# Gradient of x in a transformer block's backward: token-major against transposed accumulation, with DMA transposes back

## The chip, the cores and the metric

The kernel runs on one core of a Trainium2 chip. The time is device microseconds from launch to end, the median of several runs. The engines are named as in the profile: PE (TensorE, with its weight loads as PEld), DVE (VectorE), ACT (ScalarE), POOL (GpSimd) and SP (SyncE, which here only issues DMAs). ACT and POOL issue DMAs too, each from its own instruction queue, in order with its other work.

## The reference

One block of a transformer, forward and gradients, in bf16: S = 2048 tokens, D = 640, H = 32 heads, F = 1728.

```python
h  = x + attn(layernorm(x), wqkv, wo)     # linear attention, phi(t) = elu(t)+1
h2 = h + swiglu(layernorm(h), w1, w3, w2)
out, vjp = jax.vjp(f, x, wqkv, wo, w1, w3, w2)   # f gives h2
return out, *vjp(grad_out)                # out_0 and the gradients out_1 .. out_6
```

The change lies in `out_1`, the gradient of x. With g_q, g_k and g_v the gradients of q, k and v, and `wqkv = [wq wk wv]`:

```
g_xn = g_q wq^T + g_k wk^T + g_v wv^T          # 2048 x 640
dx   = layernorm_backward(g_xn; xn, rs) + g_h  # per token: two sums over 640, then elementwise
```

## The kernel before

Tokens lie in 16 tiles of 128 (ST = 16), the width D in 5 pieces of 128 (DT = 5); W = 512 tokens, or TPC = 4 tiles, are a chunk, of which there are SC = 4. `manual_schedule` keeps the instructions of each engine in the order of the source. A tile framework adds all semaphore waits from the reads and writes of each tile. Every step of PE, ACT, DVE, POOL and SP named below therefore runs in source order on its own engine, and waits at the head of its queue.

The kernel works in stages: forward, gradients of the second half of the block, then from about 560 us the backward of the attention. Those that bear on the change:

- The stage of g_k (L1434 to L1455, PSUM tiles `dkv`) makes `g_kT`, the gradient of k with D on the partitions. In its gaps PE does the weight gradient of q as ten `jobs` (L1357, `grad_halves` L1338): 16 matmuls each with `xnN` (the normalised x, tokens on partitions) as weights, an eviction by ACT into a piece of `obs` (L1348), a DMA out by POOL (`dmaG`).
- SP's queue before the stage of x holds DMA transposes of weights and activations (`load_xnT`, `load_pkT`, `load_wqT`), and five `e_T` (L1423 to L1425, issued at L1456): each turns one token tile of g_q (128 x 640) into a slot of `bd`.
- The stage of x (L1506 to L1517), for each of the 16 token tiles t: `e_gxn(t)` (L1489) accumulates over 15 pieces of 128 (5 of g_q from `bd`, 5 of g_k from `g_kT`, 5 of g_v from `pkT`), with the token tile as weights and 320 columns of `wqT` moving, once for each half of D, so 30 matmuls (L1495) into a two-bank PSUM tile, of which there are two. Then `ln_bwd` (L1138): ACT copies the PSUM to bf16 `gs` and sums it on the way (L1143), DVE forms the second sum and `wb` (L1146 to L1151), ACT makes `y` (L1155), DVE adds `g_h` (L1156). After that SP issues `e_T(t+5)` into the slot that PE has just left, two `k_turn` (L1485 to L1487: a DMA transpose of a 128 x 512 tile of `g_kT` into four token tiles of `g_k`, 20 in all), and the write of the 128 x 640 result (L1513). In the last tiles SP also loads the normalised h, `hn`, into `g_q` (L1483, four quarters), and the first block `gb` of the gradients of gate and up, turned by DMA (L1475, in three parts).
- After the loop ten more jobs (the weight gradient of k, with `g_k` moving) run on PE, in two PSUM banks (`njob = 2`), and their outputs leave by SP.
- The last stage (L1541 to L1549) makes the gradients of w1 and w3, 35 jobs with `hn` as weights and `gb` moving; ACT evicts each and issues its DMA, for the first six in two halves (L1547).

`ln_bwd` is shared with an earlier stage of 16 tiles (L1159), where `gs` isn't given. In that stage, between 410 and 523 us, ACT issues DMA transposes (L1168, L1268); everywhere else SP issues them.

Of the kernel before, what the change touches and what calls it, by code (L numbers as in the profile page):

```python
# [9 lines left out]
P = 128  # L10
BF16 = mybir.dt.bfloat16
F32 = mybir.dt.float32
ALU = mybir.AluOpType
AF = mybir.ActivationFunctionType
AX = mybir.AxisListType
# [5 lines left out]
ST, DT = S // P, D // P  # L21
FT, FP = 14, 1792
FL = F - 13 * P
W, SC, TPC = 512, 4, 4
HD = D // 2
NG = 27
NB = 496
# [28 lines left out]
def kernel(  # L56
# [19 lines left out]
    V, A, T, G, SY = nc.vector, nc.scalar, nc.tensor, nc.gpsimd, nc.sync  # L76
    dma, dmaT, dmaG = SY.dma_start, SY.dma_start_transpose, G.dma_start
# [8 lines left out]
    out1S = rows(out_1.flatten_outer_dims())  # L86
# [16 lines left out]
    r_v, pk_v, xn_v, hn_v, m_v, pq_v = rows(r_d), rows(pk_d), rows(xn_d), rows(hn_d), rows(m_d), rows(pq_d)  # L103
# [24 lines left out]
    bd = cp.tile([P, DT, D], BF16, name="bd")  # L128
# [44 lines left out]
    ln1, ln2 = Stats("ln1"), Stats("ln2")  # L173
# [5 lines left out]
    ps = pool("p1p", space=PSUM)  # L179
# [348 lines left out]
    for t in range(ST):  # L528
        first = None
        if t < RAW:  # L530
# [11 lines left out]
            k = p1_mm(t, D, between, kh)  # L542
            act(0, 1)
            act(1, 1)
        else:
            k = p1_mm(t, D, (lambda: p1_tr(t + 1)) if t + 1 < XT_DMA else None)
# [97 lines left out]
    ps = pool("pap", space=PSUM)  # L644
# [351 lines left out]
    for c in range(SC):  # L996
# [9 lines left out]
        for fc in range(FT):  # L1006
# [8 lines left out]
            if c == 0 and fc in (5, 7, 9, 11):  # L1015
                a, b = {5: (0, 3), 7: (3, 6), 9: (6, 10), 11: (10, 13)}[fc]
# [13 lines left out]
            if c == SC - 1 and fc in (1, 2, 5, 6):  # L1030
                i = (1, 2, 5, 6).index(fc)
# [29 lines left out]
    ps = pool("pcp", space=PSUM)  # L1061
# [18 lines left out]
    for n in range(len(blk) * DT):  # L1080
        b, m = divmod(n, DT)
        f0, fw = blk[b]
        tag = "gw0" if n // 4 in (0, 2) or n in (16, 17) else "gw1"
        acc = ps.tile([P, 512], F32, name="gw", tag=tag, bufs=4)
        for t in range(ST):
            T.matmul(acc[:, 0:fw], lhsT=g2[:, t, m * P:(m + 1) * P], rhs=hb[b][:, t, 0:fw], start=(t == 0),  # L1086
                     stop=(t == ST - 1))
# [18 lines left out]
    g_h, g_n = g_hx[:, :, G0:G0 + D], g_hx[:, :, G0 + D:]  # L1106
    n_hi = H - M_H[3][0]
    g_q = bl.tile([P, ST, D], BF16, name="g_q")
    bo = pool("bo")
    r_sb = bo.tile([P, ST, D], BF16, name="r_sb")  # L1110
    ps = pool("pbp", space=PSUM)
# [25 lines left out]

    def ln_bwd(acc, t, nrm, st, out, res, pl, gs=None, y=None):  # L1138

        if gs is None:  # L1140
            gs = pl.tile([P, D], BF16, name="gs", bufs=2)
        s = pl.tile([P, 4], F32, name="s", bufs=2)
        A.activation(out=gs[:].rearrange("p (j n) -> p j n", j=2), in_=acc[:, :, 0:HD], func=AF.Identity,  # L1143
                     accum_out=s[:, 0:1])
        wb = pl.tile([P, D], F32, name="wb", bufs=2)
        V.scalar_tensor_tensor(out=wb[:], in0=gs[:], scalar=1.0, in1=nrm, op0=ALU.mult, op1=ALU.mult,  # L1146
                               accum_out=s[:, 1:2])
        V.tensor_scalar(out=s[:, 2:3], in0=s[:, 1:2], scalar1=-1.0 / D, scalar2=None, op0=ALU.mult)
        V.tensor_scalar(out=s[:, 3:4], in0=s[:, 0:1], scalar1=-1.0 / D, scalar2=st.rs[:, t:t + 1],
                        op0=ALU.mult, op1=ALU.mult)  # L1150
        V.scalar_tensor_tensor(out=wb[:], in0=nrm, scalar=s[:, 2:3], in1=gs[:], op0=ALU.mult, op1=ALU.add)  # L1151

        def rest():
            yt = pl.tile([P, D], BF16, name="y") if y is None else y
            A.activation(out=yt[:], in_=wb[:], func=AF.Identity, bias=s[:, 3:4], scale=st.rs[:, t:t + 1])  # L1155
            V.tensor_tensor(out=out, in0=yt[:], in1=res, op=ALU.add)  # L1156
        return rest
# [72 lines left out]
    xnN = g2  # L1230
# [4 lines left out]
    xnT, pkb, gb = {}, {}, {}  # L1235
# [10 lines left out]
    for t in range(ST):  # L1246
        g = b_ghn(t)
# [13 lines left out]
        if t >= 1:  # L1261
# [3 lines left out]
            if t <= 2 * DT:  # L1265
                n = (t - 1) % DT
# [24 lines left out]
    a, b = ST - 1, ST - 2  # L1291
# [4 lines left out]
    wqT = U1.tile([P, 15, D], BF16, name="wqT", tag="D")  # L1296
# [22 lines left out]
    pkT = bv.tile([P, DT, S], BF16, name="pkT")  # L1319
# [10 lines left out]
    obs = U1.tile([P, OB], BF16, name="obs", tag="MW")  # L1330
# [3 lines left out]
    def grad_job(lhs, m, rhs, n, out, q=dma):  # L1334
        for _ in grad_halves(lhs, m, rhs, n, out, q):
            pass

    def grad_halves(lhs, m, rhs, n, out, q=dma):  # L1338

        acc = ps.tile([P, 512], F32, name="job", bufs=njob)  # L1340
        for t in range(ST):
            if t == ST // 2:
                yield
            T.matmul(acc[:, 0:n], lhsT=lhs[:, t, m * P:(m + 1) * P], rhs=rhs(t), start=(t == 0),  # L1344
                     stop=(t == ST - 1))
        ob = obs[:, cnt[0] % (OB // n) * n:(cnt[0] % (OB // n) + 1) * n]
        cnt[0] += 1
        A.copy(out=ob, in_=acc[:, 0:n])  # L1348
        for x, y, to in out:
            q(out=to, in_=ob[:, x:y])  # L1350

    def half(src, j):
        return lambda t: src[:, t, j * HD:(j + 1) * HD]

    gqkv = {0: g_q}

    def wq_jobs(ks):  # L1357
        for m in range(DT):
            for k in ks:
                for j in range(2):  # L1360
                    yield from grad_halves(xnN, m, half(gqkv[k], j), HD,
                                           [(0, HD, out2S[:, m, k * D + j * HD:k * D + (j + 1) * HD])],
                                           dma if k else dmaG)
                    yield

    ps.release()
    ps = pool("pdp", space=PSUM)
# [18 lines left out]
    def fill(n):  # L1386
        for _ in range(n):
            next(jobs, None)

    fill(4)  # L1390
    for m, (a, b) in enumerate(M_H):
        n = (b - a) * DH
        acc = ps.tile([P, 512], F32, name="gkvT", tag="dkv", bufs=3)
        for c in range(DT):
            T.matmul(acc[:, 0:n], lhsT=woT[:, c, m * P:(m + 1) * P], rhs=QT[:, c, a * DH:b * DH], start=(c == 0),
                     stop=(c == DT - 1))
# [8 lines left out]
    g_kT = bs.tile([P, DT, S], BF16, name="g_kT")  # L1405
    dx = pool("dx")
    gm, gkv_b = (dx.tile([P, DT, D], BF16, name=n) for n in ("gm", "gkv_b"))
    g_k = gqkv[1] = U1.tile([P, ST, D], BF16, name="g_k", tag="S0")
# [11 lines left out]

    gT = {}

    def e_T(t):  # L1423
        gT[t] = bd[:, t % DT, :].rearrange("p (k q) -> p k q", q=P)
        dmaT(out=gT[t], in_=g_q[:, t, :])  # L1425

    mN = U1.tile([P, DT, D], BF16, name="mN", tag="W6")
    load_pkT(2)
# [5 lines left out]
    for n in range(0, SC * DT, 2):  # L1434
        pair = [divmod(i, DT) for i in (n, n + 1)]
        acc = d_acc()
        for b, (c, d) in enumerate(pair):
            for k in range(DT):
                T.matmul(acc[:, b, :], lhsT=gm[:, k, d * P:(d + 1) * P], rhs=xnT[c][:, k, :], start=(k == 0),  # L1439
                         stop=(k == DT - 1))  # L1440
        for b, (c, d) in enumerate(pair):
            cs = slice(c * W, (c + 1) * W)
# [6 lines left out]
        if 8 <= n < 8 + 2 * DT:  # L1449
# [3 lines left out]
            ob = obs[:, k * D:(k + 1) * D]  # L1453
            unload(sq, ob)
            dmaG(out=out2S[:, i, 2 * D:3 * D], in_=ob)  # L1455
    for t in range(DT):  # L1456
        e_T(t)
    for _ in jobs:
        pass
    dx.release()  # L1460
    ba.release()


    ex = pool("ex", "right")
    hnN = g_q
    blocks = [(f0, min(f0 + NB, 2 * F)) for f0 in range(0, 2 * F, NB)]
    NB0 = 160

    def load_block(i, a=0, b=NB):
        if i < len(blocks):  # L1470
            f0, f1 = blocks[i]
            if a == 0:
                gb[i] = ex.tile([P, ST, NB], BF16, name="gb", bufs=2)
            b = min(b, f1 - f0)
            dmaT(out=gb[i][:, :, a:b], in_=gg_d[f0 + a:f0 + b, :])  # L1475
# [4 lines left out]
                for lo, out in ((0, out4S), (F, out5S)) if max(f0, lo) < min(f1, lo + F)]  # L1480

    def load_hnN(i):
        dma(out=hnN[:, i * TPC:(i + 1) * TPC, :], in_=hn_v[:, i * TPC:(i + 1) * TPC, :])  # L1483

    def k_turn(n):  # L1485
        c, d = divmod(n, DT)
        dmaT(out=g_k[:, c * TPC:(c + 1) * TPC, d * P:(d + 1) * P], in_=g_kT[:, d, c * W:(c + 1) * W])  # L1487

    def e_gxn(t):  # L1489
        acc = ps.tile([P, 2, 512], F32, name="gxn", tag="gxn", bufs=2)  # L1490
        for j in range(2):
            for k in range(15):
                ts = slice(t * P, (t + 1) * P)
                g = gT[t][:, k, :] if k < DT else g_kT[:, k - DT, ts] if k < 2 * DT else pkT[:, k - 2 * DT, ts]
                T.matmul(acc[:, j, 0:HD], lhsT=g, rhs=wqT[:, k, j * HD:(j + 1) * HD], start=(k == 0),  # L1495
                         stop=(k == 14))
        gx = scr[:, t % 2, :]
        ln_bwd(acc, t, xnN[:, t, :], ln1, gx, g_h[:, t, :], ex, scr[:, 2 + t % 2, :], scr[:, 4, :])()
        return gx

    ps.release()
    ps = pool("pep", space=PSUM)
    njob = 2
    jobs = wq_jobs((1,))
    scr = U1.tile([P, DT, D], BF16, name="scr", tag="W6")
    for t in range(ST):  # L1506
        gx = e_gxn(t)
        if t + DT < ST:
            e_T(t + DT)
        for n in (2 * t, 2 * t + 1):  # L1510
            if n < SC * DT:
                k_turn(n)
        dma(out=out1S[:, t, :], in_=gx)  # L1513
        if t > 10 and t < 15:
            load_hnN(t - 11)
        if t in (11, 13, 15):
            load_block(0, (t - 11) // 2 * NB0, (t - 9) // 2 * NB0 if t < 15 else NB)  # L1517
    load_block(1)
    for _ in jobs:
        pass  # L1520
# [20 lines left out]
    for i, (f0, f1) in enumerate(blocks):  # L1541
        n = f1 - f0
        for m in range(DT):
            last = (i, m) == (len(blocks) - 1, DT - 1)
            for a, b in ((0, n - P), (n - P, n)) if last else ((0, n),):
                c = (a + b) // 2
                halves = ((a, c), (c, b)) if i * DT + m < 6 else ((a, b),)  # L1547
                out = [(x + y - a, z + y - a, to) for y, w in halves for x, z, to in both_grads(m, f0 + y, f0 + w)]
                grad_job(hnN, m, lambda t: gb[i][:, t, a:b], b - a, out, A.dma_start)  # L1549
        load_block(i + 2)  # L1550
        if 0 < i <= 4:
            gw2_out(i - 1)
        if i < 4:
            gw2_turn(i)
# [37 lines left out]
```

## Time and profile before

| | us |
|---|---|
| median of 3 runs | 820.39 (820.0 to 820.97) |
| the profiled execution, whole | 819.31 |
| its span, first to last instruction | 817.3 |
| PE starts the stage of x | 610.84 |
| PE starts the ten jobs on g_k | 676.04 |
| PE starts the last stage | 697.77 |
| end of ACT's last issue | about 815.3 |

In the stage of x (611 to 676 us) PE is busy for all of it, DVE for 37.1 us and ACT for 25.7 us. The granted TensorE clock is full throughout. In SP's queue, the transposes of L1425 and L1487 each hold the queue for 1.2 to 1.3 us. The profile's PE times for one instruction contain its latency; the pace of a stream is read from the starts.

In the excerpts below, "L1495 PE MATMUL a<-b,c" is a line of the kernel, an engine, an operation, and what it writes and reads; "x160 | 27.0, 299 | 0.0" are count, busy us, mean ns, and idle us before. "x1, 2.5" at a DMA is the count and the median us from its issue to its landing.

### The profile page before, as it was taken

What the parts mean: (1) busy time and instruction counts of PE and PEld (TensorE: products, weight loads), DVE (VectorE), ACT (ScalarE), POOL (GpSimd) and SP (SyncE); (2) the same over time, 40 slices, a digit from 0 to 9 for tenths busy, and PEclk for the clock granted to TensorE, in tenths of its full rate; (3) what the DMA queues carried; (4) which work ended last, traced back from release to release, by engine and by line L of the source; (5) the groups of instructions that cost most, each with busy time, mean ns of one, the idle gap of its engine ahead of it and who ended that gap; (6) DMA issues with size and microseconds to landing.
All of it is one profiled execution on the core that took longest, in us unless ns stands there. A gap on an engine that the chain in (4) does not pass through costs nothing.

```text
span 817.3 us, 13571 instructions
## 1 busy us (share of the span) xinstructions
PE 812.6 (99%) x5227; PEld 495.2 (61%) x5227; DVE 444.9 (54%) x976; ACT 324.4 (40%) x607; POOL 128.6 (16%) x194
## 2 busy tenths in 40 slices
PE   9999999999999999999999999999999999999998
PEld 6777544555555555754577777777657777544444
DVE  7859997998898566300057777772565551000000
ACT  7856688665565666011122212222113442111111
POOL 2243333323222212100001111110120000000000
PEclk9999999999999999999999999999999999999999
DMA  9799899696485556999867887259995679679991
GB/s 257 210 241 283 207 264 317 203 243 175 125 211 154 169 173 168 227 263 239 242 176 182 211 198 199 58 114 180 214 184 104 122 166 255 177 179 233 239 220 38
DMA packets 334480, 159.83 MB, mean 196 GB/s; under 512 B 252304, under 2 KB 327920, under 8 KB 334416
## 3 DMA queue, kind: packets, MB, share of 16 engines
q1 hardware_dynamic: 290976, 119.37, 62.7%
q0 software_dynamic: 7008, 23.17, 8.4%
q10 hardware_dynamic: 36432, 16.42, 8.2%
q8 instruction: 41, 0.67, 0.3%
q14 instruction: 23, 0.19, 0.1%
HBM read 44.47 MB, written 53.43 MB: 120 GB/s over the span
## 4 chain that ended last, share of the span: by engine, by line
PE 98%; DVE 1%; ACT 0%; DMA 0%; POOL 0%; issue 0%
PE mm L395 21%; PE job L1344 20%; PE ghn L1131 14%; PE gxn L1495 8%; PE gw L1086 7%; PE big L268 4%; PE o L913 4%; PE o L859 3%; PE gwo L1219 3%; PE macc L430 3%; PE at L657 3%; PE gr L1188 3%; PE dkv L1439 3%; PE mm L268 1%; PE dkv L1378 1%; PE gp L395 1%
## 5 line engine op out<-in xcount | busy, mean ns | idle before, releaser
L1344 PE MATMUL job<-gb,g_q 128*128 128x496 bf16 (+3 forms) x576 | 116.8, 366 | 0.0
L1131 PEld LDWEIGHTS <-ggb 128*128 128x128 bf16 x864 | 84.5, 98 | 33.0
L395 PE MATMUL mm<-pqT,w 128*128 128x512 bf16 x405 | 93.6, 379 | 0.0
L1344 PEld LDWEIGHTS <-g_q 128*128 128x128 bf16 x576 | 55.8, 98 | 61.0
L395 PEld LDWEIGHTS <-w 128*128 128x128 bf16 x540 | 52.6, 98 | 63.0 <-issue 0.8
L1348 ACT CAST obs<-job 128x496 bf16<-128x496 f32 (+4 forms) x56 | 28.6, 511 | 136.5 <-PE job L1344 126.0
L1131 PE MATMUL ghn<-w13a,ggb 128*128 128x320 bf16 x448 | 63.5, 299 | 0.0
L1131 PE MATMUL ghn<-w13b,ggb 128*128 128x320 bf16 x416 | 61.4, 299 | 0.0
L1146 DVE SCALAR_TENSOR_TENSOR wb<-gs,hnb 128x640 f32<-128x640 bf16 x16 | 13.2, 825 | 88.1 <-ACT gs L1143 88.1
L395 PE MATMUL mm<-g2T,w2T 128*128 128x512 bf16 x240 | 59.6, 379 | 0.0
L1086 PE MATMUL gw<-hb,g 128*128 128x512 bf16 (+2 forms) x320 | 58.6, 346 | 0.0
L1086 PEld LDWEIGHTS <-g 128*128 128x128 bf16 x320 | 31.3, 98 | 26.9
L420 ACT CAST ghh<-mm 128x512 bf16<-128x512 f32 x48 | 28.1, 585 | 47.6 <-PE mm L395 41.2
L1196 POOL TENSOR_TENSOR sz<-Zb,g_h 128x640 f32<-128x640 bf16 x16 | 20.2, 1261 | 163.6 <-DVE g_h L1197 163.6
L796 ACT ACTIVATE sig<-mm 128x512 bf16<-128x512 f32 x56 | 33.7, 602 | 25.2 <-PE mm L395 21.7
L1143 ACT ACTIVATE gs<-ghn 128x640 bf16<-128x640 f32 x16 | 11.2, 703 | 77.1 <-PE ghn L1131 77.1
L395 PEld LDWEIGHTS <-w2T 128*128 128x128 bf16 x260 | 25.4, 98 | 23.4
L268 PEld LDWEIGHTS <-pqT 128*128 128x128 bf16 x320 | 30.7, 98 | 13.5 <-ACT pqT L260 0.9
L1344 PEld LDWEIGHTS <-g 128*128 128x128 bf16 x320 | 31.0, 98 | 12.8
L268 PE MATMUL big<-wqkv,pqT 128*128 128x320 bf16 x250 | 38.5, 299 | 0.2
L832 DVE TENSOR_TENSOR gate<-gate,sig 128x1024 bf16<-128x1024 bf16 x28 | 19.3, 689 | 33.8 <-ACT gate L807 31.1
L1091 ACT CAST gw2o<-gw 128x512 bf16<-128x512 f32 (+2 forms) x20 | 10.4, 519 | 65.5 <-PE gw L1086 25.5
(212 smaller groups left out, 1378.1 us busy)
## 6 DMA issues: line engine op xcount, KB each, us to landing
hh_d<-hhT SPq DMA_DIRECT2D x24, 256.0 KB, 2.8
gg_d<-gate POOLq DMA_DIRECT2D x24, 256.0 KB, 4.4
gg_d<-ghh POOLq DMA_DIRECT2D x24, 256.0 KB, 4.1
ggb<-gg_d SPq DMA_DIRECT2D x6, 896.0 KB, 5.4
ggb<-gg_d ACTq DMA_DIRECT2D x6, 832.0 KB, 5.6
ggb<-gg_d SPq DMA_DIRECT2D x2, 1728.0 KB, 12.6
x_sb<-in_A_x_dram SPq DMA_DIRECT2D x4, 640.0 KB, 5.1
pk_d<-pk_all SPq DMA_DIRECT2D x4, 640.0 KB, 5.7
```

Source lines behind the costliest of these rows:

```text
L268: T.matmul(acc, lhsT=pqT[:, c, t * P:(t + 1) * P], rhs=wqkv[:, c, n0:n0 + HD], start=(c == 0), stop=(c == DT - 1))
L395: T.matmul(acc[:], lhsT=w[:, c, fc * P:(fc + 1) * P], rhs=rhs[:, c, :], start=(c == 0), stop=(c == DT - 1))
L420: A.copy(out=ghh[n // 2][:, n % 2, :], in_=acc[:])
L430: T.matmul(macc[m][j][:, 0:n], lhsT=pk_all[:, t, m * P:(m + 1) * P], rhs=x_ext[:, t, j * HD:j * HD + n], start=(t == 0), stop=(t == ST - 1))
L657: T.matmul(at[:, 0:HD], lhsT=pqT[:, c, t * P:(t + 1) * P], rhs=Wp[:, c, j * HD:(j + 1) * HD], start=(c == 0 and not on_pe), stop=(c == DT ...
L796: A.activation(sig[:, i, :], gp[:], AF.Sigmoid)
L913: T.matmul(o2["ps"][:, 0:HD], lhsT=hhT[c][:, fc, i * P:(i + 1) * P], rhs=w2[:, fc, j * HD:(j + 1) * HD], start=(fc == 0), stop=(fc == FT - 1))
L1086: T.matmul(acc[:, 0:fw], lhsT=g2[:, t, m * P:(m + 1) * P], rhs=hb[b][:, t, 0:fw], start=(t == 0), stop=(t == ST - 1))
L1131: T.matmul(acc[:, j, 0:HD], lhsT=ggb[t // 2][:, k, lo:lo + P], rhs=rhs[:, j * HD:(j + 1) * HD], start=(k == 0), stop=(k == NG - 1))
L1344: T.matmul(acc[:, 0:n], lhsT=lhs[:, t, m * P:(m + 1) * P], rhs=rhs(t), start=(t == 0), stop=(t == ST - 1))
L1348: A.copy(out=ob, in_=acc[:, 0:n])
L1495: T.matmul(acc[:, j, 0:HD], lhsT=g, rhs=wqT[:, k, j * HD:(j + 1) * HD], start=(k == 0), stop=(k == 14))
```

## The change

The gradient of x is accumulated transposed, with D on the partitions. Group (c, d) of the 20 groups has a chunk c of 512 tokens moving and a 128 x 128 piece of `wqT` as weights: 15 matmuls of 512 columns, in one of four one-bank PSUM tiles. ACT copies the result to bf16 `gxT`, and issues a DMA transpose that writes it back as token tiles over the rows of `g_q` that the chunk came from. When the five groups of a chunk are through, their normalisation's backward runs one chunk later, from these bf16 rows: the first sum is now a `reduce_sum` on DVE, in place of ACT's copy with a sum. Its second half (`rest`, ACT's `y`, DVE's add, the write) follows one tile later still.

`e_T` now turns four token tiles of a chunk, chunk 1 and 3 into `obs`, chunk 0 and 2 into `bd`. Five `k_turn` are issued ahead of the stage, the other 15 one after each of the groups 0 to 14. The third quarter of `hn` is loaded after the groups, the fourth goes to `bd`, and the last stage reads it by `hn_row`. The last chunk's four normalisations run beside the first of the ten jobs on g_k (`fill`). In the last stage the first two outputs instead of six are split in halves.

```diff
-        s = pl.tile([P, 4], F32, name="s", bufs=2)
-        A.activation(out=gs[:].rearrange("p (j n) -> p j n", j=2), in_=acc[:, :, 0:HD], func=AF.Identity,
-                     accum_out=s[:, 0:1])
+            A.activation(out=gs[:].rearrange("p (j n) -> p j n", j=2), in_=acc[:, :, 0:HD], func=AF.Identity,
+                         accum_out=s[:, 0:1])
+        else:
+            V.reduce_sum(out=s[:, 0:1], in_=gs, axis=AX.X)
...
-    def e_T(t):
-        gT[t] = bd[:, t % DT, :].rearrange("p (k q) -> p k q", q=P)
-        dmaT(out=gT[t], in_=g_q[:, t, :])
+    def e_T(c):
+        gT[c] = (obs[:] if c % 2 else bd[:].rearrange("p k n -> p (k n)"))[:, 0:DT * W].rearrange("p (k w) -> p k w", w=W)
+        for i in range(TPC):
+            dmaT(out=gT[c][:, :, i * P:(i + 1) * P], in_=g_q[:, c * TPC + i, :])
...
-    for t in range(DT):
-        e_T(t)
+    e_T(0)
+    for n in range(DT):
+        k_turn(n)
     for _ in jobs:
         pass
+    e_T(1)
...
+    def e_gxn(c, d):
+        acc = ps.tile([P, W], F32, name="gxn", tag="gxn", bufs=4)
+        cs = slice(c * W, (c + 1) * W)
+        for k in range(15):
+            g = gT[c][:, k, :] if k < DT else g_kT[:, k - DT, cs] if k < 2 * DT else pkT[:, k - 2 * DT, cs]
+            T.matmul(acc[:], lhsT=wqT[:, k, d * P:(d + 1) * P], rhs=g, start=(k == 0), stop=(k == 14))
+        gxT = ex.tile([P, W], BF16, name="gxT", bufs=3)
+        A.copy(out=gxT[:], in_=acc[:])
+        A.dma_start_transpose(out=g_q[:, c * TPC:(c + 1) * TPC, d * P:(d + 1) * P], in_=gxT[:])
+
+    ends = []
+
+    def e_rest():
+        while ends:
+            t, rest = ends.pop()
+            rest()
+            dma(out=out1S[:, t, :], in_=scr[:, t % 2, :])
+
+    def e_ln(t):
+        rest = ln_bwd(None, t, xnN[:, t, :], ln1, scr[:, t % 2, :], g_h[:, t, :], ex, g_q[:, t, :], scr[:, 4, :])
+        e_rest()
+        ends.append((t, rest))
...
-    for t in range(ST):
-        gx = e_gxn(t)
-        if t + DT < ST:
-            e_T(t + DT)
-        for n in (2 * t, 2 * t + 1):
-            if n < SC * DT:
-                k_turn(n)
-        dma(out=out1S[:, t, :], in_=gx)
-        if t > 10 and t < 15:
-            load_hnN(t - 11)
-        if t in (11, 13, 15):
-            load_block(0, (t - 11) // 2 * NB0, (t - 9) // 2 * NB0 if t < 15 else NB)
+    for n in range(SC * DT):
+        c, d = divmod(n, DT)
+        e_gxn(c, d)
+        if DT + n < SC * DT:
+            k_turn(DT + n)
+        if c > 0:
+            if d > 0:
+                e_ln((c - 1) * TPC + d - 1)
+            else:
+                e_rest()
+        if d == DT - 1 and c + 2 < SC:
+            e_T(c + 2)
+        if n in (11, 16, 18):
+            load_hnN({11: 0, 16: 1, 18: 3}[n])
+        if n in (13, 15, 17):
+            load_block(0, (n - 13) // 2 * NB0, (n - 11) // 2 * NB0 if n < 17 else NB)
+    fill(1)
+    e_rest()
+    load_hnN(2)
+    for i in range(TPC):
+        fill(2)
+        e_ln(ST - TPC + i)
+    e_rest()
     load_block(1)
     for _ in jobs:
         pass
```

More of the change, by code (lines that the diff above doesn't have):

```diff
@@ L1138, in ln_bwd @@
     def ln_bwd(acc, t, nrm, st, out, res, pl, gs=None, y=None):
+        s = pl.tile([P, 4], F32, name="s", bufs=2)
         if gs is None:
             gs = pl.tile([P, D], BF16, name="gs", bufs=2)
-        s = pl.tile([P, 4], F32, name="s", bufs=2)
-        A.activation(out=gs[:].rearrange("p (j n) -> p j n", j=2), in_=acc[:, :, 0:HD], func=AF.Identity,
-                     accum_out=s[:, 0:1])
+            A.activation(out=gs[:].rearrange("p (j n) -> p j n", j=2), in_=acc[:, :, 0:HD], func=AF.Identity,
+                         accum_out=s[:, 0:1])
+        else:
+            V.reduce_sum(out=s[:, 0:1], in_=gs, axis=AX.X)
         wb = pl.tile([P, D], F32, name="wb", bufs=2)
@@ L1343, in grad_halves @@
                 yield
-            T.matmul(acc[:, 0:n], lhsT=lhs[:, t, m * P:(m + 1) * P], rhs=rhs(t), start=(t == 0),
+            T.matmul(acc[:, 0:n], lhsT=lhs(t)[:, m * P:(m + 1) * P], rhs=rhs(t), start=(t == 0),
                      stop=(t == ST - 1))
@@ L1360, in wq_jobs @@
                 for j in range(2):
-                    yield from grad_halves(xnN, m, half(gqkv[k], j), HD,
+                    yield from grad_halves(lambda t: xnN[:, t, :], m, half(gqkv[k], j), HD,
                                            [(0, HD, out2S[:, m, k * D + j * HD:k * D + (j + 1) * HD])],
@@ L1421, with k_turn @@
     gT = {}
-    def e_T(t):
-        gT[t] = bd[:, t % DT, :].rearrange("p (k q) -> p k q", q=P)
-        dmaT(out=gT[t], in_=g_q[:, t, :])
+    def e_T(c):
+        gT[c] = (obs[:] if c % 2 else bd[:].rearrange("p k n -> p (k n)"))[:, 0:DT * W].rearrange("p (k w) -> p k w", w=W)
+        for i in range(TPC):
+            dmaT(out=gT[c][:, :, i * P:(i + 1) * P], in_=g_q[:, c * TPC + i, :])
+    def k_turn(n):
+        c, d = divmod(n, DT)
+        dmaT(out=g_k[:, c * TPC:(c + 1) * TPC, d * P:(d + 1) * P], in_=g_kT[:, d, c * W:(c + 1) * W])
     mN = U1.tile([P, DT, D], BF16, name="mN", tag="W6")
@@ L1464 @@
     ex = pool("ex", "right")
-    hnN = g_q
     blocks = [(f0, min(f0 + NB, 2 * F)) for f0 in range(0, 2 * F, NB)]
@@ L1482, in load_hnN, with hn_row @@
     def load_hnN(i):
[L1483 to L1499, printed above, removed]
+        to = g_q[:, i * TPC:(i + 1) * TPC, :] if i < SC - 1 else bd[:, 0:TPC, :]
+        dma(out=to, in_=hn_v[:, i * TPC:(i + 1) * TPC, :])
+    def hn_row(t):
+        return g_q[:, t, :] if t < ST - TPC else bd[:, t - ST + TPC, :]
+    def e_gxn(c, d):
[17 more added lines that the diff above has]
+        ends.append((t, rest))
     ps.release()
@@ L1505 @@
     scr = U1.tile([P, DT, D], BF16, name="scr", tag="W6")
-    for t in range(ST):
-        gx = e_gxn(t)
-        if t + DT < ST:
-            e_T(t + DT)
-        for n in (2 * t, 2 * t + 1):
-            if n < SC * DT:
-                k_turn(n)
-        dma(out=out1S[:, t, :], in_=gx)
-        if t > 10 and t < 15:
-            load_hnN(t - 11)
-        if t in (11, 13, 15):
-            load_block(0, (t - 11) // 2 * NB0, (t - 9) // 2 * NB0 if t < 15 else NB)
+    for n in range(SC * DT):
+        c, d = divmod(n, DT)
+        e_gxn(c, d)
[19 more added lines that the diff above has]
+    e_rest()
     load_block(1)
@@ L1546 @@
                 c = (a + b) // 2
-                halves = ((a, c), (c, b)) if i * DT + m < 6 else ((a, b),)
+                halves = ((a, c), (c, b)) if i * DT + m < 2 else ((a, b),)
                 out = [(x + y - a, z + y - a, to) for y, w in halves for x, z, to in both_grads(m, f0 + y, f0 + w)]
-                grad_job(hnN, m, lambda t: gb[i][:, t, a:b], b - a, out, A.dma_start)
+                grad_job(hn_row, m, lambda t: gb[i][:, t, a:b], b - a, out, A.dma_start)
         load_block(i + 2)
```

## The prediction

> **What bounds the kernel now.** I read the page's busy shares and chain first, then the chain in order of time, then the stage of the change by lines, then the SP queue in that stage.
>
> ```profile
> PE 812.6 (99%) x5227; PEld 495.2 (61%) x5227; DVE 444.9 (54%) x976; ACT 324.4 (40%) x607; POOL 128.6 (16%) x194
> PE 98%; DVE 1%; ACT 0%; DMA 0%; POOL 0%; issue 0%
> ...
> 143.40 3.24 PE mm L395 x15
> ...
> 611.00 65.20 PE gxn L1495 x480
> 676.21 138.39 PE job L1344 x736
> ```
> The first two lines are of the page, the others of the chain in order of time (start, length, what). PE runs without a gap; the stage of the change is 65.20 us of L1495, and after it come the jobs of L1344, of which the first 160 (10 jobs on g_k) last from 676.04 to 697.77.
>
> ```profile
> L1495 PE MATMUL gxn<-wqT,pkT 128*128 128x320 bf16 x160 | 27.0, 299 | 0.0
> L1495 PEld LDWEIGHTS <-g_kT 128*128 128x128 bf16 x160 | 15.7, 98 | 6.1
> L1487 SPq DMA_TRANSPOSE g_k<-g_kT x20: 1217/1257/1722, 615.2 to 661.1; - x20
> DMA to landing us min/median/max: 2.5/2.5/3.6
> ghT<-g_h ACTq DMA_TRANSPOSE x14, 2.7
> gb<-gg_d SPq DMA_TRANSPOSE x9, 9.9
> ```
> A matmul's 299 ns is its latency, not its pace: 65.20/480 is 0.136 us each, and the next one starts meanwhile. Weight loads (98 ns) fit under it. A transpose of a 128x512 tile holds its queue for 1.26 us and has landed 2.5 us after its start; the second number is what a waiter sees.
>
> **PE's own work.** Removed: 480 matmuls of 320 columns, 65.2 us. Added: 300 of 512. Fifteen of these take 3.24 us (L395 above), so 20 groups take 64.8. The columns streamed are the same, 153,600; the gain is **0.4 us**. The 180 weight loads that go were hidden.
>
> **ACT, DVE, SP.** ACT loses L1143 (16 x 0.70 + 0.20) and gains 20 evictions of 0.585 (the row of L420, same shape) and 20 transpose issues of some 1.22 (L1168 on the same queue): 2.7 us a group with the activation of L1155 (0.92), under PE's 3.24. DVE gains a sum over 640 bf16: no such row; below by 0.20 (L1326, 40 elements), above by 0.82 (L1193, 640 of f32); I take 0.8, the same length. One token tile then costs DVE 2.9 to the end of L1151 and 0.49 for L1156. Beside PE this is covered. SP keeps its 16 e_T, 20 k_turn, 16 writes of out1 and 4 loads. Four splits of an output go in the last stage: ACT's queue there is idle 2.77 us of each 3.35, so nothing.
>
> **The new waits: two queues transposing in turn.** The order becomes: ACT turns block n, SP turns block n+5 of g_kT, ACT turns n+1, and so on. In this kernel's program such a change of queue is a wait for landing: the first transpose that SP issues after ACT's stretch (L1242 at 540.07) waits for the semaphores of ACT's last two (L1168, tokens 12 and 13), whose bytes it doesn't touch. It cost nothing there, for ACT's last had started at 522.14. Nowhere in this trace do the queues alternate: from 410 to 523 ACT has 24 transposes and SP none, elsewhere SP alone. So the price of a hand-over is not shown. Bounds: 1.25 us (only the issue counts) and 3.0 (median landing of L1268). I take 2.5, the landing of the same shape, plus 0.05 for the semaphore (L1527 started 0.04 after L1526's landing). [...]
>
> What queues behind it: ACT holds the next evictions, so the four PSUM banks of gxn fill and PE stops; SP holds out1, e_T and load_block. I follow T(n), ACT's issue for group n, from 610.84, PE's first gxn.
> - T(0): SP is free for e_T(0) at 601.59, as now; 4 x 1.22 and 5 k_turn x 1.26 end at 612.8. e_T(1) goes into obs, whose last reader, POOL's write at 610.92, lands 2.1 later, 613.0. Its fourth starts at 616.7 and lands 3.4 later (e_T's median there), 620.1. T(0) is at **9.3**, where the eviction alone would give 4.1.
> - T(0) to T(15): 15 hand-overs there and back, 15 x 5.1 = 76.5. At n = 4 and 9 four e_T stand behind the k_turn: 3 to 4 further issues and a landing, +5.0 and +5.5. At n = 13 the first part of block 0 does, landing in 6.7: +6.0. T(15) is at 9.3 + 76.5 + 16.5 = **102.3**.
> - T(15) to T(19): no k_turn is left. Parts two and three (landings 7.7 and 8.5, after out1's write 3.4 behind T) give 11.1 and 12.0; between them ACT alone takes 1.9 and 2.8. T(19) is at **130.1**; PE ends its last group at about 103.
> - The end: the 10 jobs' evictions stand behind T(19) on ACT, so PE does two (two PSUM banks), stops, and is released at 131 to 134. T(19) lands at 132.6. Four normalisations on DVE (4 x 2.9 + 3 x 0.5), then L1155, end at 147.6; job 4's eviction stands behind that last L1155, so job 6 starts at 148.5. Four jobs of 2.17: **157.2**.
> Today the same point is at 697.77 - 610.84 = 86.9. The last stage then runs unchanged: its loads (hn's third quarter at 140, block 0 at 127) are there by then. Sum: +70.3 us on the profiled execution's 819.3 us (span 817.3 and 2.0 around it), 889.6; the median of the runs is 1.1 above that execution, so **890**.
>
> Ends: with hand-overs of 1.25 (and landings of the other transposes at their issue times or 2.6) the same steps give +31, 851; with 3.0 and 9.9 for the block's parts, +93, 913.
>
> PE's clock is at 9 in every slice today. [...]
>
> **Rivals.**
> - *No wait between the queues* (or only on SP for ACT's, which would leave ACT free). For: nothing in the trace shows one that cost time. Against: the waits on L1242. T(n) then keeps PE's pace, T(19) is at 65.7 and lands at 68.2; but the end remains: the four normalisations finish at 82, job 4's eviction waits for them, and job 6 starts at 82.2 where PE would be ready at 77.9. +4 us: 824 (821 to 827).
> - *Not slower.* The same, and the tail is covered too: the four normalisations at the end must be done within the 13 us of six jobs after PE's last group, that is 9.6 us after T(19)'s landing, 2.4 a tile. It decides whether DVE needs under 2.4 instead of the 3.4 of my rows. Then only PE's 0.4 us counts: 820. Against: L1146, L1151 and L1156 alone are 2.2, and the sum comes on top.
> - *PE as the bound after all, transposes in turn but swallowed by the four PSUM banks.* Four banks hold 4 x 3.24 = 13 us of lag; the chain lags 65 us by the last group. Even with hand-overs of 1.25 the sum is +31; I give it nothing beyond that low end.
>
> **Chances.** The alternating waits with something like my sum: 0.82, nearly all of it in 851 to 913. No waits: 0.11. Not slower: 0.07, of it 0.02 for faster by over 0.2% (1.6 us, about what a measurement of this kernel can tell from no change), since PE has no more than 0.4 us to give. The range leaves out the two rivals and little else. The no-wait case keeps 0.03 within 0.2%. Faster 0.02, same 0.08, slower 0.90.
>
> **What would show it.** Right: in the stage ACT's and SP's transposes strictly in turn, T's starts 5.1 apart, longer steps after groups 4, 9, 13, 15 and 17; PE idle in front of gxn for ACT's evictions, and a stop of some 25 us in the g_k jobs; the stage with its jobs 157 us long instead of 87. Each step has its row: T(0) near 620, T(15) near 713, T(19) near 741. Wrong: transposes of the two queues overlapping, or PE without gaps at L1495's successor; then the wait isn't there and the time is near 824. A landing well under 2.5 when the queues are otherwise empty would bring it down towards 851.

## The result and the profile after

The changed kernel takes 880.91 us (median of 6 runs, 878.68 to 881.96) beside 820.19 for the kernel before on the same chip: a ratio of 1.0732, 95% interval [1.0715, 1.0748]. The profiled execution took 881.39 us, with a span of 879.5.

From the page of the changed kernel: busy shares, PE and its granted clock over 40 slices, the chain that ended last.

```profile
PE 827.2 (94%) x5047; PEld 481.0 (55%) x5047; DVE 455.1 (52%) x992; ACT 321.9 (37%) x595; POOL 128.7 (15%) x194
...
PE   8999999999999999999999999999876844999998
...
PEclk9999999999999999999999999999989776999999
...
PE 73%; issue 9%; DMA 7%; DVE 3%; SPq 2%; ACTq 2%; ACT 2%; POOL 1%; POOLq 0%; DVEq 0%
```

PE's share falls from 99 to 94%, nearly all of it in slices 29 to 34 (22 us each), which are the stage of x and the ten jobs after it. PE has 98% of the chain before and 73% after. The clock falls to 7 and 6 tenths in the same slices.

The chain in order of time (start, length, what), in the stage of x:

```profile
644.06 1.26 SPq L1432
...
645.37 2.46 DMA g_k<-g_kT
...
648.01 2.42 DMA g_q<-gxT
650.45 2.39 DMA g_k<-g_kT
...
652.91 1.21 ACTq L1505
...
654.77 1.21 ACTq L1505
...
656.99 1.22 ACTq L1505
...
659.73 0.35 SPq L1513
...
660.57 2.42 DMA g_k<-g_kT
...
663.06 1.21 ACTq L1505
```

The transposes of the two queues never overlap. SP's transpose (L1432) lands; ACT's (L1505) starts within 0.2 us and lands 2.42 later; then SP's next, 2.39; then ACT's. There and back is 652.91 - 648.01 = 4.90 us. Where two of ACT's follow each other, as from 652.91, the second starts 1.86 later, after one eviction. Where SP's write of a result (L1513), which waits for the activation and the add before it, stands between, there and back is longer: 663.06 - 656.99 = 6.07 us. All 20 of ACT's have one row, and the second line gives their landing:

```profile
L1505 ACTq DMA_TRANSPOSE g_q<-gxT x20: 1203/1206/1232, 627.7 to 731.8; - x20
...
DMA to landing us min/median/max: 2.4/2.4/5.0
```

PE in the same stage (start, length, what, and in brackets the idle time before it with its releaser):

```profile
634.48 1.24 PE L1502 MATMUL gxn<-obs,wqT 128*128 128x512 bf16 x5 [1.52 <-ACT gxT L1504]
...
649.90 2.29 PE L1502 MATMUL gxn<-obs,wqT 128*128 128x512 bf16 x5 [5.54 <-ACT gxT L1504]
651.98 2.30 PE L1502 MATMUL gxn<-g_kT,wqT 128*128 128x512 bf16 x5
654.12 1.24 PE L1502 MATMUL gxn<-pkT,wqT 128*128 128x512 bf16 x5
...
671.41 2.29 PE L1502 MATMUL gxn<-bd,wqT 128*128 128x512 bf16 x5 [2.26 <-ACT gxT L1504]
...
682.35 2.29 PE L1502 MATMUL gxn<-obs,wqT 128*128 128x512 bf16 x5 [5.98 <-DMA obs<-g_q]
...
713.47 4.51 PE L1346 MATMUL job<-g_k,g 128*128 128x320 bf16 x32
736.12 10.47 PE L1346 MATMUL job<-g_k,g 128*128 128x320 bf16 x64 [18.13 <-ACT obs L1350]
749.74 10.48 PE L1346 MATMUL job<-g_k,g 128*128 128x320 bf16 x64 [3.16 <-ACT obs L1350]
760.06 2.67 PE L1346 MATMUL job<-gb,g_q 128*128 128x496 bf16 x12
```

PE now waits mostly for ACT's evictions, and ACT stands behind its own transposes. Nine stops in front of gxn make 24.7 us (eight of them for evictions, one of 5.98 for `e_T`), two in the jobs 21.3. After a long stop five matmuls take 2.08 us (649.90 to 651.98) instead of 1.08, and four jobs 10.3 (749.74 to 760.06) instead of 8.7. The last stage starts at 760.06, where the kernel before had 697.77. From PE's first gxn (612.51) that is 147.55 us instead of 86.93: the stage is 60.6 longer, and it started 1.67 later. Together 62.3, and the span grew by 62.2.

### The profile page after: what moved, and what is told of

The parts are those of the page before. It is cut to its first block, busy times and chain, and to the rows that moved or that the text cites. A ratio compares the mean times of both kernels' runs of the same rounds, so it can differ in the third digit from the quotient of the medians.

```text
span 879.5 us, 13263 instructions
## 1 busy us (share of the span) xinstructions
PE 827.2 (94%) x5047; PEld 481.0 (55%) x5047; DVE 455.1 (52%) x992; ACT 321.9 (37%) x595; POOL 128.7 (15%) x194
## 4 chain that ended last, share of the span: by engine, by line
PE 73%; issue 9%; DMA 7%; DVE 3%; SPq 2%; ACTq 2%; ACT 2%; POOL 1%; POOLq 0%; DVEq 0%
PE mm L395 19%; PE job L1346 14%; PE ghn L1131 13%; PE gw L1086 7%; PE big L268 4%; PE o L913 3%; PE o L859 3%; PE macc L430 2%; DMA g_k<-g_kT 2%; PE gr L1190 2%; DMA g_q<-gxT 2%; PE at L657 2%; ACTq L1505 2%; SPq L1428 1%; DMA gb<-gg_d 1%
## 5 line engine op out<-in xcount | busy, mean ns | idle before, releaser
L1346 PE MATMUL job<-gb,g_q 128*128 128x496 bf16 (+3 forms) x432 | 93.4, 366 | 0.0
L1350 ACT CAST obs<-job 128x496 bf16<-128x496 f32 (+4 forms) x56 | 28.3, 510 | 133.4 <-PE job L1346 121.5
L1502 PEld LDWEIGHTS <-wqT 128*128 128x128 bf16 x300 | 31.5, 105 | 69.4 <-issue 41.0
L1346 PEld LDWEIGHTS <-g_q 128*128 128x128 bf16 x432 | 41.8, 98 | 45.8
L1346 PE MATMUL job<-g_k,g 128*128 128x320 bf16 x160 | 25.5, 325 | 21.3 <-ACT obs L1350 21.3
```

The costliest lines, as they stand in the source:

```text
L1346: T.matmul(acc[:, 0:n], lhsT=lhs(t)[:, m * P:(m + 1) * P], rhs=rhs(t), start=(t == 0), stop=(t == ST - 1))
L1502: T.matmul(acc[:], lhsT=wqT[:, k, d * P:(d + 1) * P], rhs=g, start=(k == 0), stop=(k == 14))
```

## The experiments

Times are compared as ratios to the kernel before, run on the same chip each time. A hundredth of it is 8.2 us.

**One queue (e1).** The changed kernel, with its 20 transposes of gxT issued by SP, like all the others:

```diff
-        A.dma_start_transpose(out=g_q[:, c * TPC:(c + 1) * TPC, d * P:(d + 1) * P], in_=gxT[:])
+        dmaT(out=g_q[:, c * TPC:(c + 1) * TPC, d * P:(d + 1) * P], in_=gxT[:])
```

> The changed kernel with one word altered: the 20 transposes of gxT are issued by SP, as all others of the stage are, so that no transpose waits for one of another queue. If the hand-overs between the two queues made the 61 us, they go at once: what is left is PE's 0.4 us and the end of the stage, where the job evictions stand behind the last L1157 on ACT, about +4 us: 823 (821 to 827), transposes on SP at PE's pace of 3.24 us a group, and no stop of PE inside the 20 groups. If instead the transposes themselves (62 of them on the DMA engines), the writes over g_q, or the normalisation one chunk behind were the cost, the time stays above 850, for all of that is unchanged.

Measured 842.88 us, 1.0268 [1.0248, 1.0288]. Putting one line's transposes on the other queue gives back 4.64% of the kernel before, 38 us of the 61, and PE runs through all 20 groups with one stop of 0.76. The hand-over is the largest cost. But the 823 expected was wrong by 20 us. The SP queue of this kernel at the end of the groups, and PE's first stop in the jobs:

```profile
676.94 1.22 SPq L1505 DMA_TRANSPOSE g_q<-gxT  x1
678.21 1.26 SPq L1432 DMA_TRANSPOSE g_k<-g_kT  x1
679.56 0.53 SPq L1513 DMA_DIRECT2D out_dram<-scr  x1
680.19 1.19 SPq L1505 DMA_TRANSPOSE g_q<-gxT  x1
...
688.47 3.89 SPq L1483 DMA_TRANSPOSE gb<-gg_d  x1
...
694.87 1.21 SPq L1505 DMA_TRANSPOSE g_q<-gxT  x1
```

```profile
693.78 6.57 PE L1346 MATMUL job<-g_k,g 128*128 128x320 bf16 x32 [10.96 <-ACT obs L1350]
```

SP has no gap from 620.91 on: a group costs it 1.21 for gxT, 1.26 for g_k and 0.53 for an output, some 3.2 us with the joins, before the e_T (5.4 a chunk) and the block's parts. That is PE's 3.24 a group already. The last transpose of gxT is issued at 694.87, 16.6 us after PE has ended its groups at 678.30; the last normalisations, and the evictions behind them, are late by as much. The queue's own issue time is the second cost.

**Four banks for the jobs (e2)**, on top of that (`njob = 2` becomes 4):

> [...] If e1 is left with a stop of PE because job 6 waits for the eviction of job 4 behind ACT's last L1157, two more banks let job 6 start on time: 819.8 to 821, within 0.2% of the kernel before. If e1's rest is something else (landing times, hn's third quarter, a slower stage), e2 equals e1.

Measured 837.6, 1.0202 [1.0185, 1.0219]: 5.4 us less by the ratios, and not the 819.8 to 821 expected. The stops in the jobs shrink from 10.96, 2.82, 0.59 and 3.63 to 6.90, 3.59 and 2.70. The two banks are worth about two jobs' time (2 x 2.17), and the late rows stay late.

**The hand-over alone, in the kernel before (e3).** Only the issuer of k_turn is changed; nothing of the change is in it:

```diff
-        dmaT(out=g_k[:, c * TPC:(c + 1) * TPC, d * P:(d + 1) * P], in_=g_kT[:, d, c * W:(c + 1) * W])
+        A.dma_start_transpose(out=g_k[:, c * TPC:(c + 1) * TPC, d * P:(d + 1) * P], in_=g_kT[:, d, c * W:(c + 1) * W])
```

> The kernel before, untouched but for one word: its 20 k_turn are issued by ACT instead of SP. Their number, their bytes and the 1.2 us that each holds a queue are the same; what is new is that e_T on SP and k_turn on ACT alternate, 20 changes of queue. If a change of queue costs a landing of 2.5 us, a token tile's round is 2.5 for e_T, 1.2 + 2.5 for two k_turn, 6.3 us against PE's 4.08; ACT's evictions stand behind it and two PSUM tiles swallow the first two tiles only: ten rounds, +15 to +20 us, 835 to 841. If hand-overs cost nothing, ACT has 25.7 + 24.4 = 50 us of work in 65 and covers it: 820 to 822.

Measured 844.88, 1.0292 [1.0274, 1.0310], some 4 us above the upper end. Its chain in order of time:

```profile
623.24 2.56 DMA bd<-g_q
625.82 1.21 ACTq L1487
627.06 2.71 DMA g_k<-g_kT
...
629.85 2.57 DMA bd<-g_q
```

A round of one transpose by SP and two by ACT takes 6.61 us here, and 6.45 to 6.82 in the others, where 6.3 was expected and PE needs 4.08 for a token tile. Ten rounds at that pace are 3 to 4 us more than expected, and PE starts the stage 1.1 later (611.94): together about what the time lies above the range. The hand-over costs in a kernel that has nothing else of the change: 24 us for 20 changes of queue.

**SP relieved (e5).** The kernel with one queue and four banks, with out1's writes and hn's loads issued by POOL, and block 0's parts moved behind the last transpose of gxT:

```diff
-        dma(out=to, in_=hn_v[:, i * TPC:(i + 1) * TPC, :])
+        dmaG(out=to, in_=hn_v[:, i * TPC:(i + 1) * TPC, :])
...
-            dma(out=out1S[:, t, :], in_=scr[:, t % 2, :])
+            dmaG(out=out1S[:, t, :], in_=scr[:, t % 2, :])
...
-        if n in (13, 15, 17):
-            load_block(0, (n - 13) // 2 * NB0, (n - 11) // 2 * NB0 if n < 17 else NB)
+    for a in range(3):
+        load_block(0, a * NB0, (a + 1) * NB0 if a < 2 else NB)
```

> As e2 (gxT's transposes on SP, four banks for the jobs), and SP is relieved: out1's writes and hn's loads are issued by POOL, and the three parts of block 0 stand behind the last transpose of gxT. In e1 PE had ended its 20 groups at 678.3, while SP's queue, full without a gap from 620.9, came to gxT's last transpose at 694.9; the four normalisations took 12.5 us more. If SP's own issue time is what is left of the loss, taking 8.5 + 2 + 9 us from it lets the last transpose start at about 680; the normalisations end at about 695, before PE needs the bank of job 4, and the time is 820 to 822, that of the kernel before. If what is left comes from the transposes' landing or from DVE, it stays at 835.

Measured 828.61, 1.0110 [1.0092, 1.0129]: 7.5 us less by the ratios, so SP's issue time was a real cost, though what each of the three moves brought was not taken apart. It is still some 7 us above the 820 to 822 expected. In its trace the last five transposes on SP are held up:

```profile
672.54 1.95 SPq L1432 DMA_TRANSPOSE g_k<-g_kT  x1
674.58 11.77 SPq L1505 DMA_TRANSPOSE g_q<-gxT  x5
```

The issue of the last ends at 686.35, 7 us after PE's groups end at 679.16, and two stops of PE in the jobs remain, 2.97 and 3.19, for evictions. In these transposes SP waits for ACT's copies into gxT: one copy waits 5.59 us for one of the three gxT buffers, and the last two stand on ACT behind activations, whose rows DVE could start only at 678.06, after waiting 7.62 for a transpose of gxT. Later, at 691.38, DVE waits 1.71 more for an output, issued by POOL, to leave its slot.

**The same with two banks (e6)** (`njob = 4` back to 2):

> As e5, with two banks for the jobs, as the change has them. This is the rival of the prediction in which no transpose waits for another queue: job 6 waits for job 4's eviction, which stands on ACT behind the last L1157: some 4.4 us above e5, 824 to 826. If the two banks cost nothing once the last transpose is on time, it equals e5.

Measured 832.8, 1.0174 [1.0145, 1.0203], 4.2 us above the one with four by the medians, 5.2 by the ratios, and above the 824 to 826 expected: the banks cost about the same on either base.

**One queue, but ACT's (e7).** The changed kernel with the stage's other transposes on ACT too:

```diff
-            dmaT(out=gT[c][:, :, i * P:(i + 1) * P], in_=g_q[:, c * TPC + i, :])
+            A.dma_start_transpose(out=gT[c][:, :, i * P:(i + 1) * P], in_=g_q[:, c * TPC + i, :])
...
-        dmaT(out=g_k[:, c * TPC:(c + 1) * TPC, d * P:(d + 1) * P], in_=g_kT[:, d, c * W:(c + 1) * W])
+        A.dma_start_transpose(out=g_k[:, c * TPC:(c + 1) * TPC, d * P:(d + 1) * P], in_=g_kT[:, d, c * W:(c + 1) * W])
...
-            dmaT(out=gb[i][:, :, a:b], in_=gg_d[f0 + a:f0 + b, :])
+            (A.dma_start_transpose if i == 0 else dmaT)(out=gb[i][:, :, a:b], in_=gg_d[f0 + a:f0 + b, :])
```

> The changed kernel with all transposes of the stage on ACT (e_T, k_turn, gxT, block 0): no change of queue in the 20 groups, but the issues stand between ACT's evictions. From e1's queue: ACT has the transposes' issues without out1 and hn (10.5 us less than SP there), and 20 evictions (11.7) and 16 of L1157 (14.7) more, so the last transpose starts at about 711 instead of 695: 855 to 860. If only the change of queue costs time and a queue's own issue time doesn't, it is at most e1's 843.

Measured 859.43, 1.0479 [1.0461, 1.0498], as expected. No hand-over is left in this kernel's groups either. ACT issues more here than in the changed kernel, and yet the time is 21 us less by the ratios: ACT's issue time alone doesn't explain the loss. It is some 17 us slower than with all on SP. ACT's evictions share the queue with 2.5 us of issues a group, and PE stops for some 29 us in all, of which the first 4.92 wait for `e_T`, which ACT issues only at 609.41, behind the evictions of the stage of g_k. Both costs are separate: the hand-over, and the queue's time.

**What held up the last transposes, taken away (e8).** The kernel with SP relieved, with five buffers for gxT, four slots for the result's rows, and hn's loads on SP again but behind the last transpose:

```diff
-        dmaG(out=to, in_=hn_v[:, i * TPC:(i + 1) * TPC, :])
+        dma(out=to, in_=hn_v[:, i * TPC:(i + 1) * TPC, :])
...
-        gxT = ex.tile([P, W], BF16, name="gxT", bufs=3)
+        gxT = ex.tile([P, W], BF16, name="gxT", bufs=5)
...
-            dmaG(out=out1S[:, t, :], in_=scr[:, t % 2, :])
+            dmaG(out=out1S[:, t, :], in_=scr[:, t % 4, :])
```

> The kernel of e5 (all transposes on SP, out1's writes on POOL, four PSUM banks for the jobs), with what held its last transposes of gxT up taken away: five buffers for gxT instead of three, four slots for the result's rows instead of two, and hn's loads back on SP behind the last transpose. If the late last transposes make up most of e5's remaining 8.5 us, the last one is issued within 4 us of PE's last group (8 in e5), the normalisations of the last chunk end about 697 instead of 704, and the time is 822 to 825. If the four last normalisations cost the time by themselves, wherever their rows come from, it stays at 827 to 830.

Measured 827.38, 1.0079 [1.0066, 1.0092]. My theory fell, and the time lies where its rival had it: the transposes did come earlier (five in 9.01 us from 674.29, the last issued some 4 us after PE's groups end at 678.14), and the gain is 2.5 us by the ratios, 1.2 by the medians, with intervals that touch; 4 to 7 were expected. DVE and PE of this kernel, in order of time:

```profile
675.00 0.82 DVE L1146 TENSOR_REDUCE s<-g_q 128x1 f32<-128x640 bf16 x1 [7.51 <-DMA g_q<-gxT]
...
677.59 0.81 DVE L1146 TENSOR_REDUCE s<-g_q 128x1 f32<-128x640 bf16 x1
...
680.57 0.81 DVE L1146 TENSOR_REDUCE s<-g_q 128x1 f32<-128x640 bf16 x1
```

```profile
687.92 6.68 PE L1346 MATMUL job<-g_k,g 128*128 128x320 bf16 x48 [0.92 <-ACT obs L1350]
694.96 2.33 PE L1346 MATMUL job<-g_k,g 128*128 128x320 bf16 x16 [0.36 <-ACT obs L1350]
700.92 7.05 PE L1346 MATMUL job<-g_k,g 128*128 128x320 bf16 x32 [3.62 <-ACT obs L1350]
```

DVE needs 2.98 us a token tile, and at 675.00 eight are still ahead of it, the four of chunk 2 and the four of chunk 3: SP issued chunk 2's last transpose at 670.49, 8.5 us after PE had ended that chunk at 661.96. Eight make 23.8 us, to 698.8. So it is not the last four by themselves, as the rival had it, but eight, which started late because chunk 2's rows came late. ACT's last activations end at 700.6, and the job evictions between them hold PE for 4.9 us.

**The jobs ahead of the tail (e9).** The last kernel, with all ten jobs placed before the last four normalisations:

```diff
+    for _ in jobs:
+        pass
     for i in range(TPC):
-        fill(2)
         e_ln(ST - TPC + i)
     e_rest()
     load_block(1)
-    for _ in jobs:
-        pass
```

> The kernel of e8, with all ten jobs on g_k placed ahead of the last chunk's four normalisations, so that on ACT no eviction of a job stands behind an activation of L1157. If that place in ACT's queue is the only thing by which the normalisation one chunk behind still costs time, PE runs through from the first group to the last job without a stop over 1 us and the time is 819.5 to 821.5, the kernel before within 0.2%. If something else stops PE there (late rows of g_k, the last stage's loads), it stays above 823, and the stop has another releaser.

Measured 825.96, 1.0067 [1.0050, 1.0083]; beside e8 the intervals overlap, so the gain of 1 us is not certain. PE:

```profile
677.45 22.07 PE L1346 MATMUL job<-g_k,g 128*128 128x320 bf16 x160
701.03 1.83 PE L1346 MATMUL job<-gb,g_q 128*128 128x496 bf16 x8 [1.51 <-DMA gb<-gg_d]
703.99 1.01 PE L1346 MATMUL job<-gb,g_q 128*128 128x496 bf16 x4 [1.13 <-DMA g_q<-hn_d]
```

The stage is as planned: from 612.70, the first gxn, to the end of the ten jobs at 699.5 PE stops nowhere, in 86.8 us; in the kernel before the same stretch, from 610.84 to 697.94, has 87.1. The time is still 0.67% above the kernel before. Its profiled execution (824.28) is 5.0 us above that of the kernel before: 2.6 are the two new stops, for block 0's last part and hn's third quarter, which now come late; 1.9 are the start of the stage, 612.70 instead of 610.84; the rest, about 0.5, lies in the last stage. No version here beats the kernel before.

Taking away the wait between the two queues while both transpose was not tried, and no run here shows what happens without it.

## Why the prediction came out as it did

The mechanism was the one forecast, its price per hand-over too; three terms of the sum were mis-sized, and in part their errors cancel: +5.9 on the first against -10.0 and -6.7 on the next two. That the total came so near is to that extent luck. From PE's first gxn, in us:

| step | predicted | measured |
|---|---|---|
| T(0), ACT's first transpose | 9.3 | 15.2 |
| T(0) to T(15) | 93.0 | 83.0 |
| T(15) to T(19) | 27.8 | 21.1 |
| T(19) to the last stage | 27.1 | 28.3 |
| sum | 157.2 | 147.6 |

- **PE's own work.** Forecast 64.8 for 20 groups and 0.4 less than before. Where nothing stops PE (e9) the groups take 677.45 - 612.70 = 64.75. Right.
- **The hand-over.** Forecast 5.1 there and back, measured 4.90 to 4.92 where nothing else stands between (627.68 to 632.60, 648.01 to 652.91, 705.73 to 710.65). Three other rounds of one transpose by each queue (from 656.99, 663.06 and 691.52) took 5.65 to 6.07, because SP's write of a result stood between them and waited for an activation and an add; in these steps the sum had nothing for it. One more (from 685.41) took 6.11, since ACT's transpose landed only after 3.61. The one queue gives back 38 us, and putting k_turn on the other queue of the kernel before costs 24. That the wait is for landing, shown before only by L1242's semaphores, is now shown in time.
- **How often.** This step failed: "the order becomes: ACT turns block n, SP turns block n+5 of g_kT". Each engine's queue does follow the source, but whose turn it is between the two queues does not. In the trace the turns are grouped: after T(0) one of SP's, then three of ACT's, then four e_T and two k_turn, one of ACT's, one of SP's, three of ACT's. From T(0) to T(19) and block 1 that makes 28 changes where the source order would have 36. Why the two queues are ordered so was not looked into. The grouping explains the first two terms: T(0) stands behind four k_turn that the source has later (SP issues five in 10.34 us from 620.96, four of them ahead of T(0)), the changes after it are fewer, and the e_T of chunk 3 come two before and two after T(10), so PE waits 5.98 us for them.
- **Block 0's parts.** Forecast landings of 6.7 to 8.5, taken from the kernel before, where SP issues on. Here they land 4.9 to 5.4 after their issue; why they are quicker was not tested. T(15) to T(16) is 8.1 where 11.1 was forecast, T(17) to T(18) 8.5 for 12.0: 6.5 us too many, nearly all of the third term. The first part, at T(13) to T(14), is 8.6 where 5.1 + 6.0 were forecast, 2.5 of the second.
- **The end.** Forecast 27.1, from four normalisations on DVE, job 4's eviction behind the last L1155 (now L1157), and four jobs. In this order it came, but the sum fits by luck: the last activation starts at 748.46, PE goes on at 749.74, 17.95 after T(19) where 18.4 was forecast. T(19) took 5.00 to land where 2.5 was forecast, and from there to PE's next job it was 12.9 where 15.9 was forecast. Of that, a tile on DVE takes 2.98 in all (e8) for 3.4, and the prediction's own terms add up to 146.6 for the end of the normalisations, not to its 147.6; its rival had 14.0 for the same stretch. The four jobs then took 10.3 us instead of 8.7, which is the clock (0.50 for the first 3.35).
- **The clock.** The sum had nothing for it. The granted clock falls from 1.00 to 0.50 with stops, and the last four jobs lose 1.6 us on the path (0.50 from 749.74 to 753.09, 1.00 from there to 760); the other half-speed stretches lie where ACT, not PE, sets the pace. The 64 matmuls from 736.12 lose as much: they take 10.47 us where 64 after no stop take 8.86 (e8, from 678.14), a loss of 1.6, which is 3.2 us at half pace; the trace has the clock at 0.50 from 736.12 to 739.44. In the changed kernel stops of 2.26 and 2.34 us were enough, while those of 0.70 and 1.52 changed nothing. Nor does the length alone decide: after a stop of 2.70 us (e2, 713.13) 32 matmuls take 4.51 us, as 32 after no stop do (e1, 678.30), and after one of 2.82 (e1, 703.16) 16 take 2.33, as after one of 0.59 (706.08).
- **The start.** Forecast as before; measured 1.67 later. The kernel before with k_turn on ACT also started 1.1 later (611.94), behind a wait of 0.27 for an eviction at L1384, which in the changed kernel is 1.00 (there L1386). But e6, which contains the change, started the stage at 610.84, as the kernel before did, and e5 at 613.36: the start varies among kernels that all have the change, and why is open.
- **The rival without waits, 824.** It can't be run as it was put. On one queue as the change has it (e1) the issues put it at 842.9. With SP relieved and two banks, as the change has them, it is 832.8 (e6). The nearest time is e8's 827.4, with four banks, and PE stopped 4.9 us by job evictions behind the normalisations, where the rival had 4. That such a tail remains was right, but no run reached 824 with it.
- **The rival "not slower".** Its condition was a tile on DVE in under 2.4 us. DVE takes 2.98 (the sum L1146 is 0.81, where I took 0.8). It falls by its own condition.

The cost in all, by the ratios: hand-overs 38 us, SP's issue time 7.5 (e5), the last transposes' delay up to 2.5 (e8), two banks instead of four 5.4 (e2), the evictions behind the tail about 1 (e9, uncertain), and 5.5 that e9 keeps, in the late loads, the later start (which varies from run to run) and what is open. The order in which they were taken off matters, since they lie over each other.

## What to carry to other kernels

Before moving DMA transposes to a second queue, see whether the two queues would alternate in time: here each change cost the landing of the last transpose, 2.4 us, not its issue of 1.2, and what stood behind it in both queues waited too. On one queue count the issue times against the stage's pace: here two transposes of 1.2 us and an output of 0.53 a group already filled PE's 3.24 us. PE, at 99%, had 0.4 us to gain from the same work in another form; what the new form put on the queues, and what stood behind it, was the whole result.

## What the runs showed of the hardware

- In the changed kernel the granted clock went from 1.00 to 0.50 with each of the seven stops of 2.26 us and more, and came back after 3 to 6 us of work at half pace (4.2 for the groups from 649.90, 5.9 for those from 682.35). A stop of 1.52 us left it at 1.00. The matmuls behind one of 1.92 in e3, of 2.70 in e2 and of 2.82 in e1 kept their full pace (in e3 five take 0.84 us, as before the stop). In these runs, then, the length of a stop alone doesn't tell whether the clock falls.
- A transpose of 128x512 within SBUF landed in 2.4 us (the median of ACT's 20). In the changed kernel two with a load of hn beside them took 3.6 and 5.0, at the same issue time of 1.2; in e8 one took 4.3 without such a load, so the cause isn't shown.
- The same write of a 128x640 row landed 1.8 us (median) after SP's issue in the changed kernel and 3.1 after POOL's with SP relieved (up to 6.5). Off the full queue the writes landed later, and yet that run (e5, which moved other issues too) was 7.5 us faster.
